# A fused attention and two-layer expert kernel on one core: the order of its instructions taken from a stored table instead of from a scheduler in the kernel

## The chip, the cores and the metric

The kernel runs on one core of a Trainium2 chip. The metric is device time in microseconds (us) from one launch. Several runs of the kernel are timed, and their median is the time; one further execution is recorded by the profiler, and all rows below come from that one.

The engines of the core are named as the profile names them: PE (matrix products), DVE (vector engine), ACT (activations), POOL (GpSimd) and SP, which here only issues DMA transfers. Each engine works through its own list of instructions in a fixed order; between engines they wait for each other by semaphores.

## The reference

Shapes: q, k, v are 4 x 8 x 576 x 64; x is then 2304 tokens x 512; d_ff is 1536.

```
scores = scale * np.matmul(q, k.transpose(0, 1, 3, 2))
mask = (rel >= 0) & (rel < window)                  # window = 64
attn = softmax(np.where(mask, scores, -1e9))
x = (attn @ v), heads joined: 2304 x 512
# layer 1
xn = x / np.sqrt(np.mean(x * x, axis=-1, keepdims=True) + 1e-06) * rms_g
g = xn @ w_gate
x = (g * (1.0 / (1.0 + np.exp(-g))) * (xn @ w_val)) @ w_out
# layer 2
gate = 1.0 / (1.0 + np.exp(-(x @ w_gate2)))
out = (gate * (x @ w_val2)) @ w_out2
```

The weights reach the chip as 64-bit floating point numbers, so the kernel converts them itself.

## The kernel before

**Attention.** There are 36 units of 64 queries for eight heads. A unit is three steps: scores (`st_s`: PE lines 383 to 390, softmax on DVE lines 396 to 400 and 404 to 406, exponentials on ACT line 403), a transposition (`st_tr`, PE line 419 and a copy on ACT line 413) and the product with v (`st_pv`, PE line 455).

**Weights.** A piece of 128 x 1024 weights arrives by one DMA of 1 MB (`w_load`, line 214): 18 pieces for layer 1 and 19 for layer 2. A piece is brought into two fp16 parts, high and low, by `w_max` (the largest magnitude, DVE line 220, and a small all-reduce on POOL line 223), `w_conv` (DVE and ACT, lines 244 to 256) and `w_split` (line 311 or 313 for the high part, line 315 on DVE for the low part). The raw pieces of layer 1 share a few slots: `w_load` of a later piece waits until line 315 has read the earlier piece of its slot.

**Layers.** The tokens go in six blocks of 384, and the 1536 hidden channels in 12 slices of 128. For a layer l, block b and slice f there are:
- `moe_g`, below G(b,f): 12 matmuls of 128 x 384 on line 551, then tanh on ACT (line 563) and in layer 1 a product on DVE (line 565), the last to read the PSUM bank of the matmuls;
- `moe_v`, below V(b,f): 12 matmuls on line 551 into the other of the two banks named `gv`, then a product on DVE (line 576 in layer 1, 578 in layer 2);
- `moe_h`: the hidden values in two fp16 parts (ACT line 592 or 596, DVE line 593 or 597);
- `moe_o`, the output product: for layer 1 twelve matmuls of 128 x 384 on lines 611 to 613, three for each of the four banks named `o`; for layer 2 nine matmuls of 128 x 512 on lines 617 to 619.

Every product needs three matmuls (high by high, high by low, low by high; `mm3`, line 551). A G or V writes into a `gv` bank and so has to wait until the DVE line (565, 576 or 578) that reads the bank's former contents is done. The first two blocks of layer 1 run while its weights are still being converted; their output products come when `w_out` is there. Ahead of each block of layer 1 stands its normalisation (`rms_first` and `split_first` for blocks 0 and 1; for the later ones `rms_sum`, lines 484 to 487 with an all-reduce on POOL, then `rms_scale` lines 521 to 525 and `rms_split` lines 532 and 533). Layer 2 starts a block with `x1_a` and `x1_b` (lines 636 to 655).

**What sets the order.** The program is traced first in the order of the source. Then `arrange` (line 942) puts it in its final order: it groups the matmuls into one tile that follow each other, gives each instruction a price (`price`), lists which instruction must follow which, and lays them down by a list schedule that runs eight times forward and eight times backward. The best of these orders is made firm by a chain of orderings along each engine, DMA issues on SP included. Tiles in pools of more than one buffer are given their buffers beforehand by `plan`; `Pool.tile` (line 54) hands them out.

Of the kernel before, what the change touches and what calls it, by code (L numbers as in the profile page):

```python
# [47 lines left out]
class Pool:  # L48
# [5 lines left out]
    def tile(self, shape, dt, name, tag=None, bufs=1):  # L54
        if bufs == 1:
            return self.pool.tile(shape, dt, tag=tag or name, name=name, bufs=1)
        l = self.asked.setdefault(tag, (bufs, []))[1]
        if self.plan is None:
            a = self.pool.tile(shape, dt, tag=tag, name=name, bufs=bufs)
        else:  # L60
            k = f"{tag}_{self.plan[tag][len(l)]}"
            if k not in self.made:
                self.made[k] = self.pool.tile(shape, dt, tag=k, name=k, bufs=1)
            a = self.made[k]
        l.append(a.name if self.plan is None else k)
        return a
# [820 lines left out]
BYTES = dict(float32=4, int32=4, uint32=4, float16=2, bfloat16=2, uint16=2)  # L887
ROUNDS = 8


def spans(x):
    b = getattr(x, "bass_ap", None)
    if b is None:
        return None
    t, ap, dt = b.tensor, [tuple(p) for p in b.ap], str(b.dtype).split(".")[-1]
    n = math.prod(c for s, c in ap[1:])
    if type(t).__name__ != "Tile":
        return None, 0, 0, 0, 0, n, dt, math.prod(c for s, c in ap) * BYTES.get(dt, 8)
    p0, f0 = divmod(b.offset, ap[0][0])
    sz = BYTES[dt]  # L900
    return t, p0, p0 + ap[0][1], f0 * sz, (f0 + 1 + sum(s * (c - 1) for s, c in ap[1:])) * sz, n, dt, 0


def price(e, i, o, n):

    op = str(i.opcode)
    big = max([x[5] for x in o + n])
    if e == "PE":
        if n[0][6] == "float32":
            t = 218.0 if o[0][5] > 64 else 112.0 if o[0][5] > 1 else 218.0  # L910
        else:
            t = 0.4225 * max(o[0][5], 128)
        return t, t + 160
    if e == "DVE":
        wide = [x for x in n if x[5] == big]
        if big <= 16:
            return 80.0, 165.0
        if op in ("Memset",):
            t = 60 + 0.84 * big
        elif op == "ISA":  # L920
            t = 150 + 0.53 * big
        elif op == "TensorReduce" or len(wide) > 1 or o[0][6] == "uint16" or str(wide[0][0].space).endswith("PSUM"):
            t = 150 + 1.07 * big
        else:
            t = 150 + 0.53 * big
        return t - 80, t
    if e == "Activation":
        t = 210 + 0.95 * big
        if o[0][6] == "uint16":
            t = 200 + 2.24 * big  # L930
        if len(o) > 1:
            t += 190
        return t - 95, t
    if e == "Pool":
        t = 1200.0 if big <= 16 else 2800.0
        return t, t
    by = max(x[7] for x in o + n)
    t = max(by / 300.0, 640.0 if by <= 131072 else 350.0)
    return t, t + 2200.0


def arrange(nc, tc):
    ops, tiles = [], {}
    last = None
    for i in nc.cur_bb.bb.instructions:
# [3 lines left out]
        o = [s for s in map(spans, i.outs) if s]  # L949
        n = [s for s in map(spans, i.ins) if s]  # L950
        occ, lat = price(e, i, o, n)
        key = o[0][0].name if e == "PE" else None
        if e == "PE" and last is not None and last[0] == (key, i.bass_priority - len(ops[last[1]]["ins"])):
            k = last[1]
        else:
            k = len(ops)
            ops.append(dict(e=ENGINES.index(e), ins=[], occ=0.0, lat=0.0, acc=[]))
        g = ops[k]
        g["ins"].append(i)
        g["lat"] = g["occ"] + lat  # L960
        g["occ"] += occ
        g["acc"] += [(True, s) for s in o if s[0] is not None] + [(False, s) for s in n if s[0] is not None]
        last = ((key, ops[k]["ins"][0].bass_priority), k) if e == "PE" else None
    N = len(ops)
    pred = [dict() for _ in ops]
    for k, g in enumerate(ops):
        for w, (t, p0, p1, f0, f1, n, dt, _) in g["acc"]:
            if t.name not in tiles:
                tiles[t.name] = {}
            blocks = tiles[t.name]  # L970
            whole = w and n * BYTES[dt] == f1 - f0
            for b in range(f0 // 1024, (f1 - 1) // 1024 + 1):
                l = blocks.setdefault(b, [])
                keep = []
                for x in l:
                    j, w2, q0, q1, g0, g1 = x
                    hit = j != k and (w or w2) and q0 < p1 and p0 < q1 and g0 < f1 and f0 < g1
                    if hit:
                        pred[k][j] = True
                    a, z = max(g0, b * 1024), min(g1, b * 1024 + 1024)  # L980
                    if not (whole and hit and p0 <= q0 and q1 <= p1 and f0 <= a and z <= f1):
                        keep.append(x)
                keep.append((k, w, p0, p1, f0, f1))
                blocks[b] = keep
    E = [g["e"] for g in ops]
    occ = [g["occ"] for g in ops]
    P = [[(j, ops[j]["lat"] + (0 if E[j] == E[k] == 0 else 35 if E[j] == E[k] else 80 if E[k] == 3 else 45)) if not (E[j] == E[k] == 0) else (j, occ[j]) for j in pred[k]] for k in range(N)]
    S = [[] for _ in ops]
    for k in range(N):
        for j, d in P[k]:  # L990
            S[j].append((k, d))

    def place(P, S, urgency, back):

        todo = [len(p) for p in P]
        heap = [(urgency[k], k) for k in range(N) if not todo[k]]
        heapq.heapify(heap)
        busy = [([], []) for _ in ENGINES]
        at, ready = [0.0] * N, [0.0] * N
        while heap:  # L1000
            _, k = heapq.heappop(heap)
            s0, e0 = busy[E[k]]
            t, d = ready[k], occ[k]
            x = bisect.bisect_right(e0, t)
            while x < len(s0) and t + d > s0[x] + 1e-6:
                t = max(t, e0[x])
                x += 1
            s0.insert(x, t)
            e0.insert(x, t + d)
            at[k] = t  # L1010
            for m, lag in S[k]:


                r = t + lag if not back else t + d + lag - occ[m]
                if r > ready[m]:
                    ready[m] = r
                todo[m] -= 1
                if not todo[m]:
                    heapq.heappush(heap, (urgency[m], m))
        return at, max(at[k] + occ[k] for k in range(N))  # L1020

    topo, todo = [k for k in range(N) if not P[k]], [len(p) for p in P]
    for k in topo:
        for m, _ in S[k]:
            todo[m] -= 1
            if not todo[m]:
                topo.append(m)
# [99 lines left out]
```

## Time and profile before

| | us |
|---|---|
| median of 3 runs | 1020.16 (1020.14 to 1020.78) |
| the profiled execution, its own time | 1016.32 |
| its span, first to last instruction | 1014.5 |
| PE busy | 959.0 (95%) |
| DVE busy | 584.4 (58%) |
| ACT busy | 409.7 (40%) |
| POOL busy | 34.9 (3%) |
| mean granted clock of PE | 0.987 of full speed |

The table is read from the top: the profiled execution took 3.84 us less than the median of the timed ones, and its span lacks 1.8 us of its own time. Busy time is time in which an engine executes; the granted clock is that of PE alone, 1.00 being the full 2.4 GHz. A stretch of the span is described by a row with the busy time of each engine in it, with the number of instructions behind an x.

### The profile page before, as it was taken

Reading aid. Unit: us, or ns where it says so; the run is one execution under the profiler, and the core shown is the slowest. Engines: PE = TensorE matmul, PEld = TensorE weight load, DVE = VectorE, ACT = ScalarE, POOL = GpSimd, SP = SyncE. Lnnn points to the kernel's source line nnn. Section 1 sums busy time; section 2 is a strip of 40 time slices with the busy share of each in tenths; the row PEclk is TensorE's granted clock in tenths of the full one; section 3 lists DMA queues with packets and bytes.
Section 4 is the critical chain, followed back from the end, with each engine's and each line's share of the span. In section 5 each row is a group of like instructions: output and inputs, shape, how many; then the busy total and the mean of one; then the engine's idle time right before and its main releaser. Section 6 shows DMA issues by size and latency. Waiting matters only on the chain.

```text
span 1014.5 us, 14919 instructions
## 1 busy us (share of the span) xinstructions
PE 959.0 (95%) x6176; PEld 583.0 (57%) x6176; DVE 584.4 (58%) x1124; ACT 409.7 (40%) x787; POOL 34.9 (3%) x40
## 2 busy tenths in 40 slices
PE   6667899789999999999999999999999999999998
PEld 6535666456655675675555555555555555555554
DVE  6989998998778888978838813212222222222221
ACT  5478867567342446344414312222222222122122
POOL 0110000100010001001001000000000000000000
PEclk9789999999999999999999999999999999999999
DMA  8455345041530220220013000000000000000000
GB/s 294 122 178 166 116 126 177 11 162 31 197 120 1 52 85 21 95 94 12 1 42 115 12 1 1 1 1 32 1 32 1 1 32 1 1 32 1 1 32 31
DMA packets 43187, 61.54 MB, mean 61 GB/s; under 512 B 23408, under 2 KB 31984, under 8 KB 38640
## 3 DMA queue, kind: packets, MB, share of 16 engines
q1 hardware_dynamic: 43120, 60.60, 18.4%
q8 instruction: 48, 0.79, 0.3%
q14 instruction: 19, 0.16, 0.1%
HBM read 55.87 MB, written 4.72 MB: 60 GB/s over the span
## 4 chain that ended last, share of the span: by engine, by line
PE 80%; DVE 14%; ACT 4%; issue 1%; POOL 0%; DMA 0%; SPq 0%; ACTq 0%; POOLq 0%
PE gv L551 47%; PE o L619 5%; PE o L618 5%; PE o L617 5%; PE o L611 4%; PE o L612 4%; PE o L613 4%; PE at L455 1%; DVE wmax L220 1%; DVE wl L256 1%; DVE th L565 1%; DVE wl L315 1%; PE at L390 1%; PE at L419 1%; PE at L387 1%
## 5 line engine op out<-in xcount | busy, mean ns | idle before, releaser
L551 PE MATMUL gv<-xhl,wl 128*128 128x384 f16 x3456 | 600.8, 329 | 31.4 <-DVE th L565 27.7
L551 PEld LDWEIGHTS <-wl 128*128 128x128 f16 x3456 | 338.6, 98 | 268.3 <-issue 45.5
L597 DVE SCALAR_TENSOR_TENSOR hh<-th,hs,hh 128x384 f16<-128x384 f32 x72 | 44.5, 618 | 238.4 <-ACT hh L596 238.4
L596 ACT ACTIVATE hh<-th,hs 128x384 f16<-128x384 f32 x72 | 44.4, 616 | 256.0 <-PE o L618 243.5
L619 PE MATMUL o<-wl,hh 128*128 128x512 f16 x216 | 81.9, 379 | 0.0
L617 PE MATMUL o<-wl,hh 128*128 128x512 f16 x216 | 81.9, 379 | 0.0
L618 PE MATMUL o<-wl,hh 128*128 128x512 f16 x216 | 81.9, 379 | 0.0
L254 ACT ACTIVATE wl<-wl 128x1024 uint16<-128x1024 uint32 (+1 forms) x32 | 78.8, 2470 | 5.4 <-DVE wl L249 5.3
L578 DVE SCALAR_TENSOR_TENSOR th<-th,gv 128x384 f32<-128x384 f32 x72 | 39.9, 554 | 68.0 <-PE gv L551 68.0
L592 ACT ACTIVATE hh<-th 128x384 f16<-128x384 f32 x48 | 25.1, 523 | 122.8 <-PE o L613 101.4
L563 ACT ACTIVATE th<-gv,tg 128x384 f32<-128x384 f32 x72 | 41.8, 581 | 57.0 <-DVE hh L593 26.3
L611 PE MATMUL o<-hh,wl 128*128 128x384 f16 x192 | 62.8, 327 | 0.0
L612 PE MATMUL o<-hh,wl 128*128 128x384 f16 x192 | 62.7, 327 | 0.0
L613 PE MATMUL o<-hh,wl 128*128 128x384 f16 x192 | 62.6, 326 | 0.0
L563 ACT ACTIVATE th<-gv,be 128x384 f32<-128x384 f32 x72 | 41.8, 580 | 48.9 <-DVE hh L597 43.2
L565 DVE SCALAR_TENSOR_TENSOR th<-th,gv 128x384 f32<-128x384 f32 x72 | 39.7, 551 | 16.9 <-ACT th L563 15.9
L593 DVE TENSOR_TENSOR hh<-th,hh 128x384 f16<-128x384 f32 x48 | 29.6, 617 | 33.0 <-ACT hh L592 32.4
L403 ACT ACTIVATE sm<-sm,nm 128x128 f32<-128x128 f32 x96 | 37.4, 391 | 17.6 <-DVE nm L400 17.5
L220 DVE TENSOR_REDUCE wmax<-wl 128x1 f32<-128x1024 f32 (+1 forms) x37 | 43.5, 1182 | 1.7 <-DMA wl<-in_moe_w_val_dram 1.7
L576 DVE SCALAR_TENSOR_TENSOR th<-th,gv 128x384 f32<-128x384 f32 x72 | 39.4, 547 | 8.2 <-PE gv L551 7.9
L613 PEld LDWEIGHTS <-wl 128*128 128x128 f16 x288 | 28.2, 98 | 18.8 <-issue 0.2
L611 PEld LDWEIGHTS <-wl 128*128 128x128 f16 x288 | 28.3, 98 | 18.3 <-issue 0.2
(168 smaller groups left out, 1040.5 us busy)
## 6 DMA issues: line engine op xcount, KB each, us to landing
wl<-in_moe_w_gate_dram SPq DMA_DIRECT2D x12, 1024.0 KB, 4.8
wl<-in_moe_w_val_dram SPq DMA_DIRECT2D x12, 1024.0 KB, 5.4
wl<-in_moe_w_out_dram SPq DMA_DIRECT2D x11, 1024.0 KB, 4.9
vn<-in_v_dram SPq DMA_DIRECT2D x28, 256.0 KB, 2.8
kt<-in_k_dram SPq DMA_DIRECT2D x15, 256.0 KB, 3.7
qbd<-in_q_dram SPq DMA_DIRECT2D x30, 128.0 KB, 3.7
out_dram<-vn SPq DMA_DIRECT2D x12, 256.0 KB, 2.0
out_dram<-sm SPq DMA_DIRECT2D x6, 256.0 KB, 2.0
```

The lines of the kernel that those rows point to most:

```text
L220: V.tensor_reduce(out=r1[:, i:i + 1], in_=wraw(layer, j + i)[:, :, 1].bitcast(F32), axis=AX.X, op=ALU.max, apply_absolute_value=True)
L254: A.activation(out=r, in_=lo, func=AF.Copy, scale=2.0 ** -29)
L551: T.matmul(pb[:, 0:n], lhsT=w_, rhs=x_, start=(c == 0), stop=(c == m - 1))
L563: A.activation(out=th[:, 0:n], in_=pg[:, 0:n], func=AF.Tanh, scale=sc)
L565: V.scalar_tensor_tensor(out=th[:, 0:n], in0=th[:, 0:n], scalar=1.0, in1=pg[:, 0:n], op0=ALU.add, op1=ALU.mult)
L597: V.scalar_tensor_tensor(out=h[:, 1, 0:n], in0=th[:, 0:n], scalar=sc, in1=h[:, 0, 0:n], op0=ALU.mult, op1=ALU.subtract)
L611: T.matmul(o[c][:, 0:n], lhsT=wh[:, cs], rhs=hi, start=st, stop=False)
L612: T.matmul(o[c][:, 0:n], lhsT=wh[:, cs], rhs=lo, start=False, stop=False)
L613: T.matmul(o[c][:, 0:n], lhsT=wl[:, cs], rhs=hi, start=False, stop=en)
L617: T.matmul(o[t], lhsT=h[:, 0, ts_], rhs=wh, start=st, stop=False)
L618: T.matmul(o[t], lhsT=h[:, 0, ts_], rhs=wl, start=False, stop=False)
L619: T.matmul(o[t], lhsT=h[:, 1, ts_], rhs=wh, start=False, stop=en)
```

## The change

The scheduler inside the kernel (`spans`, `price`, `place` and the rounds of `arrange`) is gone. A table `ORDER`, found beforehand and stored as text, now holds for each engine the order of the groups of instructions, and `arrange` only unpacks it and chains the instructions in that order. The instructions are the same, with the same tiles and addresses. In `Pool.tile`, tiles that have a tag but one buffer (`pT` and `xf`) now also go through the plan. The new file is shorter, but its kernel body stands two lines lower: line 551 before is line 553 now.

```
@@ Pool.tile
-        if bufs == 1:
-            return self.pool.tile(shape, dt, tag=tag or name, name=name, bufs=1)
+        if tag is None:
+            return self.pool.tile(shape, dt, tag=name, name=name, bufs=1)
...
-ROUNDS = 8
...
-def price(e, i, o, n):
...
+ORDER = (
+    'c-n<l349Y}7N7UcB$F?9(kpFg8q(6%UR+vH5JV`TESCs~2rh!+>f%uq4`ex1Ks-2fm$M!Va)}2Zh#ZR?MOKtU%27*8Q+m+!O4^)FGT%-bn#_dy'
...
+)
...
 def arrange(nc, tc):
...
-    for r in range(ROUNDS):
-        at, end = place(P, S, urgency, False)
...
+        key = i.outs[0].bass_ap.tensor.name if e == "PE" else None
+        if e != "PE" or last != (key, i.bass_priority - len(ops[-1][1])):
+            ops.append((e, []))
+            last = (key, i.bass_priority)
+        ops[-1][1].append(i)
...
+    d = zlib.decompress(base64.b85decode(ORDER))
+    n = len(d) // 2
+    assert n == len(ops)
+    seq = list(itertools.accumulate(struct.unpack(f"{n}h", bytes(x for y in zip(d[:n], d[n:]) for x in y))))
...
+    before = None
+    for k in seq:
+        for i in ops[k][1]:
+            if before is not None and before.engine == i.engine:
+                tc.add_manual_dep(i, before.name, mybir.DependencyInfo(mybir.DependencyClass.NoSync, mybir.DependencyReason.DATA), reason="order")
+            before = i
```

Three places show what the table does. In the rows, a name is a tile: `o_...`, `at_...` and `gv_...` are PSUM banks, `xhl_...` the split tokens of a block, `th_...` and `hh_...` hidden values, and `wl_73` and `wl_74` the two large areas that hold weights, raw or converted.

**The start of DVE.** Behind the clearing of buffers, DVE had the softmax of the first units, before:

```order
L396 TENSOR_REDUCE nm_140<-o_134 128x4
L397 TENSOR_SCALAR nm_140<-nm_140 128x4
L396 TENSOR_REDUCE nm_157<-o_151 128x4
L397 TENSOR_SCALAR nm_157<-nm_157 128x4
L404 TENSOR_SCALAR su_143<-su_143 128x4
L405 RECIPROCAL su_143<-su_143 128x4
L396 TENSOR_REDUCE nm_184<-o_174 128x4
L406 TENSOR_TENSOR wl_74<-wl_74,su_143 128x512
```

and now:

```order
L745 MEMSET warm_92 128x1
L764 MEMSET mhalf 128x1
L246 TENSOR_SCALAR wl_73<-wl_74 128x1024
L222 TENSOR_REDUCE wmax_401<-wl_74 128x1
L249 TENSOR_SCALAR wl_73<-wl_73 128x1024
L251 TENSOR_SCALAR wl_74<-wl_74 128x1024
L254 TENSOR_SCALAR wl_74<-wl_74 128x1024
...
L226 TENSOR_SCALAR amax<-amax 128x2
L227 TENSOR_SCALAR pw<-amax 128x2
L230 TENSOR_SCALAR isc<-pw 128x2
L398 TENSOR_REDUCE nm_157<-o_151 128x4
```

The first two weight pieces of layer 1 are converted ahead of the first row of a softmax (line 396, now 398), which comes at place 20. SP follows suit: its first transfer was k, and the first weight piece came at place 11 of its list and the second at 13; now weight pieces stand at places 1, 3, 8 and 12, with k, q and the constants between.

**PE around V(1,10) of layer 1.** `xhl_617` (now `xhl_616`) is block 1 and `xhl_2050` is block 2. Before, V(1,10) followed a G of block 2, and the output products of block 0 began behind it:

```order
L551 MATMUL gv_168<-xhl_2050,wl_73 128x384
L551 LDWEIGHTS wl_73
L551 MATMUL gv_205<-xhl_617,wl_73 128x384
...
L611 LDWEIGHTS wl_73
L611 MATMUL o_174<-wl_74,wl_73 128x384
L612 LDWEIGHTS wl_73
L612 MATMUL o_174<-wl_74,wl_73 128x384
L613 LDWEIGHTS wl_73
L613 MATMUL o_174<-wl_74,wl_73 128x384
```

and now, between G(1,11) and V(1,10):

```order
L553 LDWEIGHTS wl_73
L553 MATMUL gv_168<-xhl_616,wl_73 128x384
L613 LDWEIGHTS wl_73
L613 MATMUL o_134<-wl_74,wl_73 128x384
L614 LDWEIGHTS wl_73
L614 MATMUL o_134<-wl_74,wl_73 128x384
L615 LDWEIGHTS wl_73
L615 MATMUL o_134<-wl_74,wl_73 128x384
L553 LDWEIGHTS wl_73
L553 MATMUL gv_205<-xhl_616,wl_73 128x384
```

Three output matmuls of block 0 stand right ahead of V(1,10), and 66 others stand earlier still: of the 12 x 12 = 144 output matmuls of block 0, none was ahead of V(1,10) and now 69 are. The eight score matmuls of attention unit 20 have also come ahead of it, and G(2,0) has gone behind it. On DVE, 400 instructions had to be done before V(1,10) could start, and now 411.

**DVE where the normalisation of block 3 begins.** Lines 484 to 486 (now 486 to 488) make the squares and their sums, and POOL's all-reduce (line 487) starts right behind them. Line 593 (now 595) makes the low part of a hidden slice. Before:

```order
L484 TENSOR_TENSOR xhl_238<-xf 128x1536
L485 TENSOR_TENSOR xhl_238<-xhl_238 128x768
L486 TENSOR_TENSOR xhl_238<-xhl_238 128x384
L247 TENSOR_SCALAR wl_74<-wl_74 128x1024
L593 TENSOR_TENSOR hh_2269<-th_567,hh_2269 128x384
L565 SCALAR_TENSOR_TENSOR th_567<-th_567,gv_168 128x384
L576 SCALAR_TENSOR_TENSOR th_631<-th_631,gv_205 128x384
```

and now:

```order
L486 TENSOR_TENSOR xhl_238<-xf_538 128x1536
L487 TENSOR_TENSOR xhl_238<-xhl_238 128x768
L567 SCALAR_TENSOR_TENSOR th_480<-th_480,gv_168 128x384
L401 SCALAR_TENSOR_TENSOR sm_437<-at_228,masks 128x512
L488 TENSOR_TENSOR xhl_238<-xhl_238 128x384
L402 TENSOR_REDUCE nm_184<-sm_437 128x4
L249 TENSOR_SCALAR wl_74<-wl_74 128x1024
L578 SCALAR_TENSOR_TENSOR th_630<-th_630,gv_205 128x384
L249 TENSOR_SCALAR wl_74<-wl_74 128x1024
L595 TENSOR_TENSOR hh_2326<-th_630,hh_2326 128x384
```

Between the last sum and the next hidden slice there stood one instruction (line 247), and now there are four.

## Rows read from the trace of the kernel before

A G or a V is a row with line 551 and 12 matmuls, or the first of them where the row holds more or fewer; blocks and slices don't stand in the rows, but follow from the order of the program.

**Rows 1.** The page: busy time of each engine, then the chain that ended last.
```profile
PE 959.0 (95%) x6176; PEld 583.0 (57%) x6176; DVE 584.4 (58%) x1124; ACT 409.7 (40%) x787; POOL 34.9 (3%) x40
...
PE 80%; DVE 14%; ACT 4%; issue 1%; POOL 0%; DMA 0%; SPq 0%; ACTq 0%; POOLq 0%
```

**Rows 2.** Windows by stage: length, busy time by engine (instructions), granted clock, DMA share, GB/s.
```profile
0.00:20.00 20.00, 12.59 (x93) 11.40 (x93) 10.83 (x29) 9.45 (x38) 0.19 (x4) 1.00 0.87 263
...
300.00:510.00 210.00, 206.55 (x1449) 132.40 (x1449) 176.41 (x315) 92.39 (x210) 8.68 (x9) 0.99 0.14 44
...
576.00:1001.00 425.00, 424.95 (x2416) 236.10 (x2414) 96.73 (x171) 94.80 (x160) 0.64 (x1) 1.00 0.03 10
...
40.00:60.00 20.00, 12.58 (x55) 8.27 (x56) 17.20 (x28) 10.52 (x9) 3.67 (x1) 0.72 0.56 162
...
0.00:4.42 4.42, 0.00 (x0) 0.00 (x0) 2.95 (x7) 1.28 (x1) 0.19 (x4) 1.00 0.43 104
```

**Rows 3.** Waits of PE, 0 to 230 us: total, times, longest.
```profile
PE gv L551 <- DVE th L565: 22.7, 12, 5.6
...
PE o L383 <- DMA wl<-const: 6.1, 1, 6.1
```

**Rows 4.** Windows: the stretch up to the start of V(1,10).
```profile
0.00:207.83 207.83, 161.07 (x1220) 113.04 (x1221) 185.29 (x401) 140.93 (x283) 15.38 (x18) 0.94 0.46 145
```

**Rows 5.** Timeline of PE around 61 and 208 us: start, length, what, idle before.
```profile
61.39 4.00 PE L551 MATMUL gv<-xhl,wl 128*128 128x384 f16 x12 [5.56 <-DVE th L565]
...
207.83 2.11 PE L551 MATMUL gv<-xhl,wl 128*128 128x384 f16 x12 [1.74 <-DVE th L576]
209.78 0.33 PE L611 MATMUL o<-wl,wl 128*128 128x384 f16 x1
```

**Rows 6.** Timeline of DVE, 8 to 17 us.
```profile
8.48 0.69 DVE L396 TENSOR_REDUCE nm<-o 128x4 f32<-128x512 f32 x1 [4.06 <-PE o L387]
...
14.47 0.66 DVE L396 TENSOR_REDUCE nm<-o 128x4 f32<-128x512 f32 x1
15.05 0.68 DVE L406 TENSOR_TENSOR wl<-wl,su 128x512 f32<-128x512 f32 x1
...
15.90 0.17 DVE L404 TENSOR_SCALAR su<-su 128x4 f32<-128x4 f32 x1
16.11 0.18 DVE L405 RECIPROCAL su<-su 128x4 f32<-128x4 f32 x1
```

**Rows 7.** Timeline of SP: the first transfer issued.
```profile
0.72 0.68 SPq L345 DMA_DIRECT2D kt<-in_k_dram  x1
```

**Rows 8.** DMA issues of the whole span: count, KB each, median us to landing.
```profile
wl<-in_moe_w_gate_dram SPq DMA_DIRECT2D x12, 1024.0 KB, 4.8
wl<-in_moe_w_val_dram SPq DMA_DIRECT2D x12, 1024.0 KB, 5.4
```

**Rows 9.** The same, issues of the first 25 us.
```profile
wl<-in_moe_w_gate_dram SPq DMA_DIRECT2D x2, 1024.0 KB, 8.9
wl<-in_moe_w_val_dram SPq DMA_DIRECT2D x2, 1024.0 KB, 10.9
```

**Rows 10.** Waits of PE, 215 to 640 us.
```profile
PE gv L551 <- DVE th L565: 4.9, 4, 2.1
```

**Rows 11.** Timeline of all engines, 296.5 to 302 us.
```profile
297.19 2.78 POOL L487 PARTITION_ALL_REDUCE xhl<-xhl  x1 [9.78 <-DVE xhl L486]
297.51 2.02 DVE L593 TENSOR_TENSOR hh<-th,hh 128x384 f16<-128x384 f32 x1
```

**Rows 12.** Timeline of PE, around 301 and 308 us.
```profile
300.79 3.56 PE L551 MATMUL gv<-xhl,wl 128*128 128x384 f16 x12 [2.07 <-DVE th L565]
...
308.15 0.33 PE L613 MATMUL o<-hh,wl 128*128 128x384 f16 x1
308.45 1.78 PE L551 MATMUL gv<-xhl,wl 128*128 128x384 f16 x10
```

**Rows 13.** Timeline of DVE, around 270 us.
```profile
270.56 1.22 DVE L220 TENSOR_REDUCE wmax<-wl 128x1 f32<-128x1024 f32 x1 [1.69 <-DMA wl<-in_moe_w_val_dram]
```

More of the change, by code (lines that the diff above doesn't have):

```diff
@@ L1 @@
-import bisect
-import heapq
+import base64
+import itertools
 import math
+import struct
+import zlib
 from contextlib import ExitStack
@@ L886 @@
 ENGINES = ["PE", "DVE", "Activation", "Pool", "SP"]
-BYTES = dict(float32=4, int32=4, uint32=4, float16=2, bfloat16=2, uint16=2)
-ROUNDS = 8
[L891 to L901, printed above, removed]
@@ L942, in arrange @@
 def arrange(nc, tc):
-    ops, tiles = [], {}
-    last = None
+    ops, last = [], None
     for i in nc.cur_bb.bb.instructions:
@@ L948, in arrange @@
             continue
[L949 to L1027, printed above, removed]
-    assert len(topo) == N, "a circle"
-    tail = [0.0] * N
-    for k in reversed(topo):
-        tail[k] = max([tail[m] + d for m, d in S[k]], default=occ[k])
-    best = None
-    urgency = [float(k) for k in range(N)] if START == "trace" else [-x for x in tail]
-    log = []
-    for r in range(ROUNDS):
-        at, end = place(P, S, urgency, False)
-        log.append(round(end))
-        if best is None or end < best[0]:
-            best = (end, at)
-        back, e2 = place(S, P, [-(at[k] + occ[k]) for k in range(N)], True)
-        log.append(round(e2))
-        urgency = [e2 - back[k] - occ[k] for k in range(N)]
@@ L1043, in arrange @@
-    if VERBOSE:
-        print("arranged", N, log)
-    end, at = best
-    for e in range(len(ENGINES)):
-        before = None
-        for k in sorted((k for k in range(N) if E[k] == e), key=lambda k: (at[k], k)):
-            for i in ops[k]["ins"]:
-                if before is not None:
-                    tc.add_manual_dep(i, before.name, mybir.DependencyInfo(mybir.DependencyClass.NoSync, mybir.DependencyReason.DATA), reason="order")
-                before = i
-    return ops, at, P
-VERBOSE = False
@@ L1057 @@
-START = "tail"
+        key = i.outs[0].bass_ap.tensor.name if e == "PE" else None
[3 more added lines that the diff above has]
+        ops[-1][1].append(i)
+        if e != "PE":
+            last = None
+    d = zlib.decompress(base64.b85decode(ORDER))
+    n = len(d) // 2
+    assert n == len(ops)
+    seq = list(itertools.accumulate(struct.unpack(f"{n}h", bytes(x for y in zip(d[:n], d[n:]) for x in y))))
@@ L1060 @@
+    assert sorted(seq) == list(range(n)) and [ops[k][0] for k in seq] == sorted((e for e, _ in ops), key=ENGINES.index)
+    before = None
[4 more added lines that the diff above has]
+            before = i
 _INS = ['q', 'k', 'v', 'moe_w_gate', 'moe_w_val', 'moe_w_out', 'moe_rms_g', 'moe2_w_gate', 'moe2_w_val', 'moe2_w_out']
```

70 lines of the change are left out of this document (36 added, 34 removed).

## The prediction

> **What bounds the kernel now.** The page comes first. PE is busy for 95% of the span and holds 80% of the chain that ended last; DVE holds 14% of it [rows 1]. So PE is the bound on average, and the question is where it is not. The windows by stage answer that: from 576 to 1001 us PE is busy for 424.95 of 425 us, while it has 12.59 of 20 us at the start [rows 2]. What can be won lies ahead of 576 us, and most of it ahead of 218 us.
>
> Up to 230 us PE's waits are nearly all of one kind: a G or V whose `gv` bank line 565 has not yet read, 22.7 us in 12 waits, the longest 5.6 [rows 3]. DVE explains them: in the first 207.83 us it is busy for 185.29 us, PE for 161.07 and ACT for 140.93 [rows 4]. There DVE is the bound: it converts the weights, and PE can go no faster than DVE lets the banks free. V(1,10) starts at 207.83 us after 1.74 us of waiting for DVE [rows 5]; what PE does from then on waits for little. So the end is set by two numbers: **how late DVE is when V(1,10) may start**, and **how much of PE's work is done by then**.
>
> At full rate twelve matmuls of 128 x 384 start to start take 209.78 - 207.83 = 1.95 us, 162.5 ns each [rows 5]. DVE's price depends on the order too. An instruction that needs nothing of the one before it starts before that one ends (14.47 + 0.66 = 15.13, the next at 15.05: 0.08 us gained); one that needs its direct predecessor starts after it (15.90 + 0.17 = 16.07, the next at 16.11: 0.04 us lost) [rows 6]. Over the whole trace the medians of such pairs are -0.081 us (915 pairs) and +0.035 us (208 pairs). A direct dependence so costs 0.116 us.
>
> **The change part by part.** No instruction is added or taken away, so every term is a shift.
>
> *1. Work moved ahead of V(1,10).* On PE 69 output matmuls of block 0 come ahead of it (69 x 0.1625 = 11.2 us) and 8 score matmuls of unit 20 (0.22 us each in the trace, 1.8), and the 12 of G(2,0) go behind it (1.95): 11.0 us more of PE's work is done by then. On DVE 16 instructions come ahead (two weight pieces' conversion and the softmax of units 18 and 19; 11.25 us by their durations in the trace) and 5 go behind (3.0): 8.2 us more. But of the 400 DVE instructions there 74 waited on their direct predecessor, and of the 411 now 37 do. By start to start that is 8.2 - 11 x 0.081 - 37 x 0.116 = 3.0 us. So PE has 11.0 us less to do behind a gate that opens 3.0 us later: **8.0 us gained**. The bounds are 2.8, if DVE pays full durations, and 11.0. I take 8.0, since the overlap is in the rows.
>
> Here the Trainium skill speaks against the change: "VectorE: DVE Perf Modes", section "The DRAIN you can't avoid", says that the next operation does not start until the pipe is empty and that leaving semaphores out gains nothing. By that this term would be 2.8 us. The trace disagrees with it by the 0.116 us above; the same section also says that an operation which nothing holds starts earlier, and the trace agrees with that.
>
> *2. DVE's start.* In the first 20 us DVE is busy for 10.83, so idle for 9.17 [rows 2]: it waits 4.06 us for the first scores [rows 6], which wait for the constants till 6.1 us [rows 3]. Now it converts weights meanwhile. Its buffers are cleared at 8.48 - 4.06 = 4.42 us [rows 6]. SP's first issue stands at 0.72 [rows 7] and is now a weight piece; over the span such a piece lands 4.8 to 5.4 us after its issue [rows 8], so at 5.5 to 6.1. DVE waits 1.1 to 1.7 us for it, the idle time ahead of 4.42 (4.42 - 2.95 = 1.47 us [rows 2]) stays, and 1.3 us I leave for short waits behind the first piece: 4.2 instead of 9.2 us idle, **5 us gained**. The other bound: in the first 25 us the pieces take 8.9 and 10.9 us [rows 9], which would leave about 1 us. Those stood behind ten other transfers, so I go by the row of the span. PE's own start is later, since k and the constants stand behind the weights; it has 30.2 us of work ahead of G(0,0) where DVE now has 60, so that is covered.
>
> *3. Idle time within DVE's stretch.* From 20 to 207.83 us DVE is idle for 207.83 - 185.29 - 9.17 = 13.4 us [rows 2, 4], in short waits for ACT, PE and POOL. The new order puts other work between most dependent pairs, but five refills of raw weight slots are now used after only 5.8, 7.8, 6.5, 6.5 and 5.9 us of DVE work from the instruction that frees the slot, where before no refill had under 9.7. With landings of 4.8 to 5.4 us they just hold. I take **2 us gained**, of bounds 6 and -3.
>
> *4. Late stops of PE.* From 215 to 640 us PE waits 4.9 us for DVE, 2.07 and 2.08 of it at G(2,8) and G(4,8) [rows 10, 12]. The chain behind: line 593 took 2.02 us instead of 0.56 while POOL's all-reduce ran from 297.19 for 2.78 us [rows 11]; tanh and line 565 came late, and then PE's clock fell, so that the twelve matmuls took 3.56 instead of 2.11 us [rows 5, 12]. Besides, 22 G's between 308 and 576 us started late by the step from 308.15 to 308.45 less 0.1625, 0.14 us [rows 12]: 3.1 us. Together 4.9 + 1.45 + 3.1 = 9.4 us. Now other work stands between the last sum and line 595 in block 3, and there is more PE work between a bank's fill and its next use. What the new order leaves thin are some 20 places in layer 2 with only three matmuls as cover; at 0.14 us each and one half stop they cost 2.8 us at most. I take 2.4: **7 us gained**. Bounds 0 (other DVE instructions now run under the all-reduce; in block 5 a line 595 still directly follows the sums) and 9.4.
>
> **Sum.** 8 + 5 + 2 + 7 = 22 us. Against the profiled execution, 1016.3 - 22 = 994.3 us. The median of the runs lies 3.84 us above that execution; on its basis 1020.2 - 22 = **998 us**.
>
> **The rivals.**
>
> *A. Only the moved work counts.* The first weights land as slowly as in [rows 9], the refills eat the inner gains, and the late stops come back under other instructions, as half of them may. Then 8 + 1 + 0 + 0 = 9 us: 1011. For it: PE's waits go back to DVE again and again, so whatever frees one exposes the next. Against it: DVE's work ahead of any PE place is at most 30 us more than PE's own now, where it was 36 at V(1,10).
>
> *B. DVE pays full durations.* Then term 1 is 2.8 instead of 8: 1003 us. For it: 0.04 us are lost, not gained, at each direct dependence [rows 6], and 37 of them are left; against it: the 915 pairs that overlap. The section of the Trainium skill that is named under term 1 would bring it about.
>
> *C. Slower: weights come too late.* The five short refills stand between 25 and 210 us, where DVE is the bound, so each us of a late piece is a us of the end. In the trace of before DVE once waited 1.69 us for a piece that stood behind other transfers [rows 13], and in the crowded start a piece took 10.9 us [rows 9]. A refill that takes both, 12.6 us, against a mean cover of 6.5, costs 6.1 us; five of them 30 us: 998 + 30 = 1028 us. It decides once the five together lose over 22 us, which is at landings of 10.9. Against it: the landings of the span [rows 8].
>
> *D. The change does nothing much.* The order of the table may be one that hardly differs where it counts, or the renamed tiles and 81 more waiting instructions on ACT take it back (at the 0.04 us of a dependent step [rows 6], 3.2 us, on an engine that is idle for 67 of 207.83 us [rows 4]). Then 1017 to 1021.
>
> PE's clock is a risk on both sides: it is granted 0.72 between 40 and 60 us [rows 2], where twelve matmuls take 4.00 us [rows 5]; as long as DVE is the bound there, this costs nothing.
>
> **How the numbers follow.** About 2 us, 0.2%, is what a measurement of this kernel can tell from no change. My forecast, with its own range of 985 to 1004, has a chance of 0.56; A 0.20; B 0.10; C 0.09; D 0.05. Faster is the forecast with A and B, 0.86; the same is D, 0.05; slower is C, 0.09. The low end, 985, takes terms 2 to 4 at their good bounds (6 + 6 + 9, with term 1 at 8, is 29: 991) and term 1 at 11 with some 3 us more for waits that vanish altogether. The high end, 1012, takes in A. Left out are C and D and a little at the low end.
>
> **What would show it right or wrong.** In the new profile the first G starts near 64 us instead of 47.6, yet V(1,10) starts near 204 us with 11 us more of PE's work done; DVE is idle for about 4 of the first 20 us and for some 15 us up to V(1,10), not 22.5; a G with 2 us of waiting right behind POOL's long all-reduce is rare; and from 576 us on PE has no gap. Term 1 is wrong if DVE's steps don't get shorter start to start. Rival C shows as DVE waiting for DMA by line 222 in the waits, and A as PE waits of over 5 us behind 215 us.

## The result and the profile after

| | before | changed |
|---|---|---|
| median of four runs each | 1020.25 us (1020.14 to 1020.78) | 996.5 us (995.46 to 997.68) |
| ratio, 95% interval | | 0.9767 (0.9750 to 0.9783) |
| the profiled execution, its own time | 1016.32 | 997.35 |
| its span | 1014.5 | 995.6 |

The change makes the kernel 23.75 us faster by the medians and 19.0 us by the profiled executions. Executions of one kernel scatter by some us here (the kernel before took 1015.97 to 1020.78 us over the whole study, and its profiled execution is among the fastest), so totals are compared by medians and ratios below, and stretches within one profile.

The page of the changed kernel, first the busy times, then the chain that ended last:

```profile
PE 958.7 (96%) x6176; PEld 587.7 (59%) x6176; DVE 579.0 (58%) x1124; ACT 404.9 (41%) x787; POOL 31.7 (3%) x40
...
PE 89%; DVE 5%; DMA 3%; ACT 2%; issue 1%; SPq 1%; DVEq 0%; ACTq 0%
```
PE is as busy as before, in 19 us less; of the chain, DVE's share fell from 14% to 5% [rows 1].

The windows by stage, with the columns of [rows 2], then the stretches up to the first G and up to V(1,10):

```profile
0.00:20.00 20.00, 8.52 (x51) 7.75 (x52) 16.80 (x30) 7.05 (x15) 0.92 (x5) 1.00 0.99 301
...
300.00:510.00 210.00, 209.65 (x1474) 133.19 (x1473) 174.98 (x313) 92.99 (x194) 11.96 (x10) 1.00 0.14 43
...
576.00:990.00 414.00, 413.38 (x2322) 226.93 (x2320) 90.68 (x160) 91.76 (x155) 0.35 (x1) 1.00 0.03 10
...
0.00:204.78 204.78, 174.18 (x1293) 125.74 (x1294) 188.63 (x414) 146.97 (x302) 11.08 (x18) 0.91 0.52 164
0.00:68.85 68.85, 40.11 (x304) 35.21 (x305) 60.50 (x143) 45.84 (x102) 4.39 (x9) 0.75 0.69 214
```
In the first 20 us DVE is idle for 3.20 us, not 9.17, and PE does less (8.52 us, not 12.59). From 300 to 510 us PE lacks 0.35 us of being always busy, not 3.45 [rows 2]. In layer 2 it lacks 0.62 us, where before it lacked 0.05 (the ends of matmuls are modelled, so short delays show only in part). Up to V(1,10), DVE is busy for 188.63 of 204.78 us; before it was 185.29 of 207.83 [rows 4].

The timeline of PE at the first G (36 matmuls without a gap), at V(1,10) and at V(1,11):

```profile
68.85 6.01 PE L553 MATMUL gv<-xhl,wl 128*128 128x384 f16 x36
...
204.78 2.11 PE L553 MATMUL gv<-xhl,wl 128*128 128x384 f16 x12
...
207.66 0.65 PE L553 MATMUL gv<-xhl,wl 128*128 128x384 f16 x3
```
V(1,10) starts 3.05 us earlier than before [rows 5], with 11.05 us more of PE's work done: 14.1 us are won by then. The first G, at 68.85 us, is 21 us later than in the kernel before.

Waits of PE, from 68 to 230 us and then from 215 us to the end:

```profile
PE gv L553 <- DVE th L567: 1.8, 2, 1.5
...
PE gv L553 <- DVE th L578: 1.5, 1, 1.5
PE gv L553 <- DVE th L567: 0.3, 1, 0.3
```
Before, the first kind took 22.7 us up to 230 us and 4.9 us behind it [rows 3, 10].

The windows from 40 us to V(1,10) show when PE became the bound:

```profile
40.00:60.00 20.00, 12.01 (x75) 10.65 (x75) 17.35 (x45) 15.92 (x33) 0.00 (x0) 0.50 0.45 144
60.00:68.85 8.85, 7.59 (x62) 6.21 (x62) 7.54 (x26) 4.84 (x7) 1.09 (x1) 0.59 0.41 151
68.85:100.00 31.15, 29.65 (x220) 19.92 (x220) 28.75 (x63) 27.25 (x60) 0.77 (x3) 1.00 0.48 153
100.00:140.00 40.00, 39.91 (x308) 28.07 (x306) 38.25 (x92) 32.71 (x57) 1.45 (x3) 0.96 0.48 152
140.00:204.78 64.78, 64.51 (x468) 42.53 (x467) 61.14 (x121) 41.16 (x85) 4.47 (x4) 1.00 0.39 123
```
From 68.85 us on PE is busy for 134.07 of 135.93 us, and DVE for 128.14. Both engines are nearly full there. Most of what PE lost by V(1,10), it lost ahead of 68.85 us, where DVE was busy for 60.50 us and PE's clock fell to half.

**The account of lost time.** The table takes the start of a PE instruction less the full-rate time of all PE work ahead of it (162.5 ns for a 128 x 384 matmul, 216 ns for 128 x 512, and so on): the time that PE had lost when so much of its work was done. It is worked out from the trace and the order of each kernel; the other columns belong to runs below.

| PE work done, us | before | changed | new to 112, then old | new to 272, then old | old to 286, then new | old layer 2 and one swap |
|---|---|---|---|---|---|---|
| 60 | 48.1 | 47.5 | 48.1 | 48.2 | 50.8 | 45.5 |
| 160 | 65.7 | 51.9 | 65.3 | 52.6 | 68.4 | 48.6 |
| 220 | 66.7 | 53.2 | 66.3 | 53.9 | 70.3 | 49.9 |
| 540 | 80.6 | 58.9 | 80.5 | 69.0 | 76.4 | 54.8 |
| 900 | 80.5 | 61.7 | 80.4 | 68.9 | 79.2 | 54.7 |

Three parts can be read from the first two columns: 13.5 us are won by 220, another 8.2 us between 220 and 540 (the rest of layer 1), and 2.9 us are lost again in layer 2. Against this execution of the kernel before, nothing is won by 60: the gain is made between 60 and 160 us of work.

The first row depends on the execution, though: the old order had lost 50.8 us by 60 in another one (old to 286), and the changed kernel, run again, had lost 45.4. From 60 to 900 its two executions lost 14.2 and 14.6 us, the kernel before 32.4. So gains of an order are best read from 60 on.

### The profile page after: what moved, and what is told of

It is laid out like the page before. It is cut to its first block, busy times and chain, and to the rows that moved or that the text cites. A ratio compares the mean times of both kernels' runs of the same rounds, so it can differ in the third digit from the quotient of the medians.

```text
span 995.6 us, 14971 instructions
## 1 busy us (share of the span) xinstructions
PE 958.7 (96%) x6176; PEld 587.7 (59%) x6176; DVE 579.0 (58%) x1124; ACT 404.9 (41%) x787; POOL 31.7 (3%) x40
## 4 chain that ended last, share of the span: by engine, by line
PE 89%; DVE 5%; DMA 3%; ACT 2%; issue 1%; SPq 1%; DVEq 0%; ACTq 0%
PE gv L553 55%; PE o L619 5%; PE o L621 5%; PE o L613 5%; PE o L620 5%; PE o L615 4%; PE o L614 4%; PE at L457 2%; PE at L389 1%; DMA wl<-in_moe_w_val_dram 1%; PE at L391 1%; PE at L392 1%; DMA wl<-in_moe_w_gate_dram 1%; PE at L421 1%; DMA qbd<-in_q_dram 1%
## 5 line engine op out<-in xcount | busy, mean ns | idle before, releaser
L553 PE MATMUL gv<-xhl,wl 128*128 128x384 f16 x3456 | 590.4, 326 | 4.4 <-DVE th L567 2.1
L553 PEld LDWEIGHTS <-wl 128*128 128x128 f16 x3456 | 337.5, 98 | 236.0 <-issue 10.3
L256 ACT ACTIVATE wl<-wl 128x1024 uint16<-128x1024 uint32 (+1 forms) x32 | 78.6, 2474 | 14.6 <-DVE wl L251 14.5
L615 PEld LDWEIGHTS <-wl 128*128 128x128 f16 x288 | 28.2, 98 | 18.6
L613 PEld LDWEIGHTS <-wl 128*128 128x128 f16 x288 | 28.3, 98 | 17.4
L614 PEld LDWEIGHTS <-wl 128*128 128x128 f16 x288 | 28.2, 98 | 17.1
```

The lines of the kernel that those rows point to most:

```text
L256: A.activation(out=r, in_=lo, func=AF.Copy, scale=2.0 ** -29)
L553: T.matmul(pb[:, 0:n], lhsT=w_, rhs=x_, start=(c == 0), stop=(c == m - 1))
L613: T.matmul(o[c][:, 0:n], lhsT=wh[:, cs], rhs=hi, start=st, stop=False)
L614: T.matmul(o[c][:, 0:n], lhsT=wh[:, cs], rhs=lo, start=False, stop=False)
L615: T.matmul(o[c][:, 0:n], lhsT=wl[:, cs], rhs=hi, start=False, stop=en)
```

## The experiments

All are the changed file with another table; the instructions are the same in every one, and none leaves out work. My theory was that of the prediction: an early part (DVE's start and work moved ahead of V(1,10)) and a late part, which add up.

**Is it the order alone?**

```
 ORDER = (
-    the table of the change
+    the order of the kernel before, written as a table
 )
```

> The order of the kernel before, written as a table into the changed kernel; everything else of the change stays (the unpacking, the renamed one-buffer tiles). My theory, that only the order of the instructions counts: 1020.2 us, within 1.5. Rival, that the renamed tiles and the waits that come with them take part in the gain or cost something: off from 1020.2 by 3 us or more, either way.

Measured: 1017.51 us beside 1018.51 for the kernel before, ratio 0.9995 (0.9980 to 1.0011). (The expected 1020.2 was the median of another series.) The renamed tiles cost and gain nothing that can be measured. That rules out my rival D's second half, and lets the old order stand for the kernel before in what follows.

**The two halves, first attempt.** The table takes one order up to a time, with all that this needs, and the rest in the other.

```
+    new order for what it starts before 232 us; then the old order        (first part)
+    old order for what it starts before 235 us; then the new order        (last part)
```

> The new order for all that the changed kernel starts in its first 232 us (with all that this needs), then the rest in the order of before. My theory, two separate gains: what PE has won by 232 us (13.7 us) stays, the late part (8.0 us won in layer 1, 2.9 lost in layer 2) goes: 1020.2 - 13.7 = 1006.5 us, 1004 to 1009. Rival 1, all of the gain is made ahead of 232 us: 997. Rival 2, the early gain is taken back because the late order of before makes PE wait for the same DVE work a little later: over 1012.

> The reverse: the order of before for its first 235 us, then the rest in the new order. My theory: the late part alone, 8.0 won and 2.9 lost, 1020.2 - 5 = 1015 us, 1012 to 1017. Rival 1, the late order only works when DVE is ahead early: 1019 or slower. Rival 2, most of the gain is late: under 1008.

Measured: first part 1010.5 us, ratio 0.9917 (0.9889 to 0.9946); last part 1018.55 us, ratio 0.9999 (0.9987 to 1.0011). Both missed. PE's waits behind the seam show why. In the first part, on the timeline:

```profile
244.99 3.46 PE L553 MATMUL gv<-xhl,wl 128*128 128x384 f16 x12 [6.00 <-DVE th L567]
```
and in the last part, in the list of waits behind 215 us:

```profile
PE at L457 <- ACT pT L415: 3.6, 3, 2.0
```
Each kernel waits right at its seam, since one order there expects work that the other had not done yet. So the totals measured the seam as well, and told nothing on the question.

**The two halves, at a better seam.** The seam now lies where both orders have done nearly the same work.

```
+    new order for what it starts before 272 us; then the old order
+    old order for what it starts before 286 us; then the new order
```

> The new order for all that the changed kernel starts in its first 272 us, then the order of before. At 232 us the two orders had done different things (24 us of PE and DVE work that only one of them had behind it), and the first attempt lost 9.3 us of PE's time right at that seam; at 272 us (286 us in the kernel before) they differ by 6 us. My theory, separate gains: 13.5 us are won by then and stay, the late part is lost as before: 23.7 - 8.0 + 2.9 = 18.6, or by stretches 13.5 to 18 us under the kernel before, ratio 0.982 to 0.987. Rival, that the early gain is taken back by the late order wherever the seam lies: ratio 0.99 or more, as in the first attempt.

> The order of before for its first 286 us, where the two orders differ by 6 us of work, then the new order. My theory: the late part alone, 14.2 us of PE's late time become 5.1 in layer 1, and 2.8 are lost in layer 2: 5 to 6.3 us under the kernel before, ratio 0.9938 to 0.995. Rival, that the late order needs DVE ahead: ratio 0.999 or more, as in the first attempt with the seam at 235 us.

Measured: new to 272, 1004.05 us beside 1018.58, ratio 0.9855 (0.9834 to 0.9876); old to 286, 1012.24 us beside 1018.81, ratio 0.9941 (0.9921 to 0.9962). Both are as expected: 14.5 and 6.6 us, in sum 21.1, where the whole change gave 22.4 us beside the second of them. The late part's 6.6 is an upper figure: its executions had a mean granted clock of 0.981 to 0.988, those of the kernel before beside them 0.978 to 0.983. By the account of lost time, from 60 us of work on, the early part gains 11.7 us and the late one 4.0, in sum 15.7 of 18.2. In the main the two are separate gains.

**Within the early part: the output products.**

```
 PE, around V(1,10) of layer 1
-    69 output matmuls of block 0 ahead of V(1,10)
     V(1,10)
+    the 69 output matmuls
```

> The new order, but on PE the 69 output matmuls of block 0 that it had moved ahead of V(1,10) stand right behind V(1,10) again; DVE, ACT, POOL and SP are as in the changed kernel. In its trace DVE lets V(1,10) go at 203.1 us and V(1,11) at 207.5, and PE reaches them at 204.8 and 207.7. My theory, that these matmuls fill PE while DVE is behind: PE waits at V(1,10) until about 203.1, then has 11.2 us of outputs ahead of V(1,11): about 9.5 us lost, 996.5 + 9.5 = 1006 us, 1003 to 1008. Rival, that the gain comes from DVE's early start and PE would have had the matmuls' time anyway: 996 to 998.

Measured: 1008.05 us (1005.02 to 1010.26), 11.6 us over the changed kernel, ratio to the kernel before 0.9889 (0.9868 to 0.9909). On PE's timeline the waits for DVE are back:

```profile
187.31 2.11 PE L553 MATMUL gv<-xhl,wl 128*128 128x384 f16 x12 [1.68 <-DVE th L567]
194.62 3.89 PE L553 MATMUL gv<-xhl,wl 128*128 128x384 f16 x12 [5.19 <-DVE th L567]
...
205.13 2.11 PE L553 MATMUL gv<-xhl,wl 128*128 128x384 f16 x12 [0.99 <-DVE th L578]
```
By the account of lost time, from 60 to 900 us of work, this kernel lost 23.7 us and the changed one 14.2, which is 9.5 more. So whether all of the matmuls' 11.2 us were lost, or the 9.5 that I expected, is not settled. The rows do settle the place: not V(1,10) alone waits, but already two G's ahead of it, and at the second the twelve matmuls took 3.89 us instead of 2.11. My expectation named the wrong place, and the mechanism stands: these matmuls fill PE while DVE is behind.

**Within the early part: DVE's start.**

```
+    new order for what it starts before 112 us; then the old order
```

> The new order for all that the changed kernel starts in its first 112 us, a place where the two orders have done nearly the same work (the new one 6.8 us of DVE and 2.8 us of PE more), then the order of before. My theory: this is the start's gain alone, 6 to 7 us under the kernel before, ratio 0.993 to 0.994. Rival 1, an earlier DVE start is lost again at the next wait: ratio 0.998 or more. Rival 2, the start is what the whole early gain comes from: 13 us, ratio 0.987.

Measured: 1015.87 us (1012.78 to 1018.9), ratio 0.9970 (0.9956 to 0.9985), beside 1018.81: 3 us, half of what I expected. (The account of lost time compares single executions and shows no gain by 900, 80.4 against 80.5.) Windows of this kernel:

```profile
0.00:20.00 20.00, 8.57 (x46) 7.70 (x47) 16.84 (x30) 7.09 (x15) 0.92 (x5) 1.00 0.99 303
...
112.00:150.00 38.00, 33.79 (x236) 22.66 (x233) 30.56 (x79) 22.24 (x43) 0.37 (x1) 1.00 0.34 110
```
the same stretch of the changed kernel:

```profile
112.00:150.00 38.00, 37.91 (x286) 27.07 (x284) 36.41 (x91) 28.54 (x54) 1.80 (x4) 0.96 0.48 154
```
and in the list of DVE's waits up to 208 us:

```profile
DVE th L567 <- ACT th L565: 7.7, 8, 2.6
```
DVE does start early (16.84 us busy of 20) and has then 7.4 us without work between 112 and 150 us. In the old order it meets the products of G's that PE has not come to; 7.7 us go in such waits, where the kernel before has some 2. So an early start of DVE does not give its full price without an order behind it that gives both engines work. The reverse, the moved output products without the early start, was not run.

**The late stops: POOL's all-reduce.** On DVE, blocks 3 and 5, with the lines of the changed file (block 3 shown):

```
 L487 TENSOR_TENSOR xhl_238<-xhl_238 128x768
+L595 TENSOR_TENSOR hh_2256<-th_566,hh_2256 128x384
 L488 TENSOR_TENSOR xhl_238<-xhl_238 128x384
-L249 TENSOR_SCALAR wl_74<-wl_74 128x1024
-L595 TENSOR_TENSOR hh_2256<-th_566,hh_2256 128x384
 L567 SCALAR_TENSOR_TENSOR th_566<-th_566,gv_168 128x384
 L578 SCALAR_TENSOR_TENSOR th_630<-th_630,gv_205 128x384
+L249 TENSOR_SCALAR wl_74<-wl_74 128x1024
```

> The order of before, but on DVE in blocks 3 and 5 of layer 1 the low part of the hidden slice goes ahead of the last sum and the 128 x 1024 weight instruction behind the two products that read PSUM, so that nothing with two SBUF inputs and no large SBUF-only instruction stands between POOL's long all-reduce and the products that PE waits for. My theory, that the all-reduce holds such instructions up: PE waits some 0.5 instead of 2.1 us at G(2,8) and G(4,8), and the slow clock behind the first stop goes: 4 us, 2.5 to 5.6, under the order of before (ratio 0.994 to 0.998). Rival, that PE waits there for another reason: ratio 0.999 to 1.001, the stops stay.

Measured: 1016.0 us beside 1018.58, ratio 0.9978 (0.9964 to 0.9991). The timeline of this kernel:

```profile
296.81 0.56 DVE L595 TENSOR_TENSOR hh<-th,hh 128x384 f16<-128x384 f32 x1 [0.47 <-ACT hh L594]
297.29 0.55 DVE L488 TENSOR_TENSOR xhl<-xhl 128x384 f32<-128x384 f32 x1
...
298.02 0.55 DVE L567 SCALAR_TENSOR_TENSOR th<-th,gv 128x384 f32<-128x384 f32 x1 [0.18 <-ACT th L565]
298.04 2.74 POOL L489 PARTITION_ALL_REDUCE xhl<-xhl  x1 [10.69 <-ACT th L565]
...
298.62 2.11 PE L553 MATMUL gv<-xhl,wl 128*128 128x384 f16 x12
...
298.95 1.30 DVE L249 TENSOR_SCALAR wl<-wl 128x1024 int32<-128x1024 int32 x1
...
480.11 2.11 PE L553 MATMUL gv<-xhl,wl 128*128 128x384 f16 x12 [1.62 <-DVE th L567]
```
Line 595 takes 0.56 us, G(2,8) starts without a wait at 298.62, and what now stands under the all-reduce, line 249, takes 1.30 us instead of the 0.69 that it takes elsewhere. Both stops of [rows 10, 12] are gone. In block 5 another came behind them (1.62 us at 480.11: the normalisation's chain, which now starts earlier, stands ahead of line 595 there), so the gain is 2.6 us, at the lower end.

The changed kernel has the same thing in other clothes. Its timeline:

```profile
291.10 2.74 POOL L489 PARTITION_ALL_REDUCE xhl<-xhl  x1 [15.84 <-DVE xhl L488]
...
291.42 1.90 DVE L249 TENSOR_SCALAR wl<-wl 128x1024 int32<-128x1024 int32 x1
...
293.24 0.54 DVE L578 SCALAR_TENSOR_TENSOR th<-th,gv 128x384 f32<-128x384 f32 x1
...
293.83 1.46 PE L553 MATMUL gv<-xhl,wl 128*128 128x384 f16 x8 [1.54 <-DVE th L578]
```
Line 249 under the all-reduce takes 1.90 us, and the product of V(2,5) stands behind it; PE waits 1.54 us.

**Layer 2, and a faster kernel.**

```
+    new order through layer 1 (its first 563 us); then the old order
```

> The new order through layer 1 (all that the changed kernel starts in its first 563 us), then layer 2 in the order of before. In the changed kernel PE starts 14 times late by 0.13 to 0.25 us in layer 2, where three output matmuls cover the release of a bank; the order of before has nine there. My theory: those 2.8 us come back, 996.5 - 2.8 = 993.7 us. Rival, that the old layer 2 does not fit behind the new layer 1 and waits at the seam: 996 or slower.

and then, besides, on DVE in block 3:

```
 L402 TENSOR_REDUCE nm_184<-sm_437 128x4
-L249 TENSOR_SCALAR wl_74<-wl_74 128x1024
 L578 SCALAR_TENSOR_TENSOR th_630<-th_630,gv_205 128x384
+L249 TENSOR_SCALAR wl_74<-wl_74 128x1024
 L249 TENSOR_SCALAR wl_74<-wl_74 128x1024
```

> As the kernel with the old layer 2, and on DVE in block 3 the product of V(2,5) goes ahead of a 128 x 1024 weight instruction that took 1.90 instead of 0.69 us under the all-reduce in the changed kernel (PE waited 1.54 us for it). My theory: 1.5 us less than the kernel with the old layer 2, some 992.2 us, the fastest of all. Rival, that the wait moves to the next instruction: as that kernel.

Measured: 994.05 us (992.56 to 995.28), ratio 0.9759 (0.9739 to 0.9778), with the old layer 2; 991.43 us (990.52 to 994.98), ratio 0.9740 (0.9719 to 0.9761), with the swap too. The first came as expected. The second is by its median the fastest kernel of the study, some 5 us under the changed one, but the two intervals overlap, and the swap explains little of the step between them: the spans of the two profiled executions differ by 4.8 us, and 4.4 of these were lost ahead of 60 us of PE's work (49.9 and 45.5), where both have the same order. From 60 to 900 the two lost 9.6 and 9.2 us. The layer 2 of the second kernel, and its all-reduce of block 3:

```profile
560.00:985.00 425.00, 424.95 (x2402) 234.74 (x2400) 93.95 (x166) 95.31 (x160) 0.64 (x1) 1.00 0.03 10
```
```profile
287.20 2.74 POOL L489 PARTITION_ALL_REDUCE xhl<-xhl  x1 [15.22 <-DVE xhl L488]
...
288.07 0.56 DVE L578 SCALAR_TENSOR_TENSOR th<-th,gv 128x384 f32<-128x384 f32 x1 [0.47 <-PE gv L553]
...
288.55 1.95 DVE L249 TENSOR_SCALAR wl<-wl 128x1024 int32<-128x1024 int32 x2
...
292.52 2.11 PE L553 MATMUL gv<-xhl,wl 128*128 128x384 f16 x12 [0.59 <-DVE th L578]
```
PE lacks 0.05 us in layer 2, and the product of V(2,5) (288.07) no longer waits behind line 249. PE's wait there, 0.9 us with the old layer 2 alone, is gone, and one of 0.59 us came a little later: the rival, that the wait moves on, holds in the main.

**What a direct dependence costs.** The changed kernel was run once more beside it.

> The changed kernel once more, as the measure for the run with direct dependences on the same chip: 995 to 998 us.

At 23 places on DVE, of this kind:

```
 L398 TENSOR_REDUCE nm_140<-o_151 128x4
-L251 TENSOR_SCALAR wl_74<-wl_74 128x1024
 L399 TENSOR_SCALAR nm_140<-nm_140 128x4
+L251 TENSOR_SCALAR wl_74<-wl_74 128x1024
```

> The new order, but on DVE at 23 places ahead of V(1,10) two neighbours are exchanged so that an instruction again stands right behind the one it needs: 69 of the 411 instructions then wait on their direct predecessor instead of 37, and no instruction comes more than one place later. My theory, that each such dependence costs DVE 0.116 us: 3.7 us more DVE time, and with PE's slack of 0.1 to 0.2 us at G(1,10) and V(1,11) 2.5 to 3.7 us more for the kernel than the changed one. Rival, that DVE drains behind every instruction anyway (the rule of the Trainium skill's page VectorE: DVE Perf Modes, section The DRAIN you can't avoid): no difference, within 1 us.

Measured: 996.43 us for the changed kernel, 997.32 (996.8 to 999.95) with the dependences back; ratios 0.9779 (0.9760 to 0.9799) and 0.9794 (0.9774 to 0.9815). The time settles nothing: 0.9 us lies inside the intervals, under the 2.5 that I expected, and within what the rival allows. The traces do settle the price of one place. Up to 204 us, 69 instructions that needed their direct predecessor started 0.035 us behind its end, by the median, and 318 others 0.082 us ahead of it; in the changed kernel 37 and 342 did, at the same two values. They do not bear out the sum, 32 x 0.116 = 3.7 us: DVE's instructions 141 to 411, from about the first G to V(1,10), took 130.9 us without their waits of over 0.07 us, and 129.1 in both executions of the changed kernel. That is 1.8 us more; why not 3.7 stays open. The waits of PE from 68 to 230 us, with the dependences back and then without:

```profile
PE o L508 <- DVE xhl L507: 2.0, 1, 2.0
PE gv L553 <- DVE th L567: 0.3, 1, 0.3
```
```profile
PE gv L553 <- DVE th L567: 0.7, 2, 0.4
```
PE waits 2.3 us instead of 0.7, and by the account it lost 16.4 us from 60 to 900 us of work, where the changed kernel lost 14.2 and 14.6.

## Why the prediction was right, and where it was not

Predicted were 998 us, 985 to 1012, with faster at 0.86; measured are 996.5. The sum of the terms was made against the profiled execution: 22 us predicted, 19.0 measured.

One reading behind it was too wide. Up to 230 us PE's waits in the kernel before sum to 46.7 us, and the 22.7 that the prediction calls nearly all are half of them; 17.6 lie ahead of the first G. No term rests on it.

**Term 1 (8.0 us).** PE had 11.05 us more behind it at V(1,10), as counted, and DVE was busy for 188.63 - 185.29 = 3.3 us longer, predicted 3.0. It is right in size, and putting the matmuls back cost 11.6 us, or 9.5 by the account. Rival B falls: DVE was busy 3.3 us longer, not 8.2, and the prices of 0.035 and -0.082 us hold in three traces. The rule of the Trainium skill behind it ("VectorE: DVE Perf Modes", "The DRAIN you can't avoid": the next operation waits until the pipe is empty, semaphores or not) does not agree with these traces, where 342 instructions started 0.082 us ahead of the end before them, by the median; what the section adds, that an operation which nothing holds starts earlier, does agree.

**Term 2 (5 us).** The first weight was there at 5.83 us, 1.39 us after DVE was ready for it, and DVE had its first scores at 14.17 us, having converted weights till then:

```profile
5.83 0.69 DVE L246 TENSOR_SCALAR wl<-wl 128x1024 f32<-128x1024 f32 x1 [1.39 <-DMA wl<-in_moe_w_gate_dram]
...
14.17 0.69 DVE L398 TENSOR_REDUCE nm<-o 128x4 f32<-128x512 f32 x1 [0.17 <-PE o L389]
```
DVE's idle time in 20 us fell by 9.17 - 3.20 = 6.0 us. So the size was right, and the step that failed is that I added it as a term of its own: run alone, the new start was worth 3 us, since the old order behind it made DVE wait for PE. With the new order behind it and only the outputs put back, 14.5 - 11.6 = 2.9 us of the early part were left, near 6.0 + 0.4 (term 3) - 3.3 = 3.1. So term 2 holds only together with the order of term 1; whether term 1 needs the early start, no run shows.

**Term 3 (2 us).** Between 20 us and V(1,10) DVE was idle for 204.78 - 188.63 - 3.20 = 12.95 us; 13.4 before. It gave 0.4. Rival C is what took the rest, in small; among DVE's waits up to 215 us stand

```profile
DVE wmax L222 <- DMA wl<-in_moe_w_gate_dram: 1.9, 1, 1.9
...
DVE wmax L222 <- DMA wl<-in_moe_w_val_dram: 1.2, 1, 1.2
```
which is 3.1 us of waiting for refilled weights. It never came near the 22 us from which C would have decided. The size of this term changes from execution to execution: when the changed kernel ran again, V(1,10) started at 202.77 us,

```profile
0.00:202.77 202.77, 173.63 (x1293) 124.41 (x1294) 188.43 (x414) 146.89 (x302) 11.07 (x18) 0.91 0.52 166
```
DVE was idle for 3.06 us in the first 20, and for 202.77 - 188.43 - 3.06 = 11.28 us from there on, 0.8 of them for a refill. There term 3 gave 2.1 us, as predicted.

In the first execution the three together: 6.0 + 0.4 - 3.3 = 3.1 us earlier at V(1,10), as the row shows (3.05), and 11.05 of work: 14.1, predicted 15.

**Term 4 (7 us).** By the account of lost time 8.2 us were won in layer 1, where I had hoped for nearly all of 9.4, and 2.9 lost in layer 2, where I took 2.4, and 2.8 at most for layer 2 and half a stop together: 5.3 in all. That sum was wrong, since 20 x 0.14 is 2.8 by itself and leaves nothing for the half stop. So what is missing is the stop at 293.83 us: I had named the chance that other DVE instructions would come under the all-reduce, and it is not in the sum. In layer 2 PE starts 14 times late by 0.13 to 0.25 us; one of them:

```profile
755.32 0.38 PE L621 MATMUL o<-wl,hh 128*128 128x512 f16 x1
755.78 1.95 PE L553 MATMUL gv<-xhl,wl 128*128 128x384 f16 x11
```
The last of three matmuls starts at 755.32, the next V at 755.78 instead of 755.54. I gave 0.14 us each for 20 places; it is nearly the same sum. My list of signs contradicted that term, though: it said that PE would have no gap from 576 us on.

**What bounds the kernel.** I had V(1,10) as the gate that counts. It is so in the kernel before. In the changed one PE runs without notable waits from its first G on, so most of what is lost is lost ahead of 68.85 us. I had put that G near 64 us. In the last 8.85 us ahead of it PE was busy for 7.59 at a granted clock of 0.59, so a slow clock may cost time there. My sentence that it costs nothing while DVE is the bound overlooks that a low clock can make DVE wait for PE. (Its row, the 4.00 us at 61.39, also lies behind the window that it names.) The old order shows it, in the kernel before and then in the last-part run, which has the same order up to 235 us:

```profile
28.00:47.60 19.60, 12.63 (x98) 11.49 (x99) 18.56 (x45) 9.35 (x10) 1.78 (x1) 0.77 0.36 107
```
```profile
28.00:47.60 19.60, 14.80 (x86) 13.33 (x87) 15.63 (x40) 7.33 (x9) 1.77 (x1) 0.50 0.28 75
...
49.98 4.37 PE L553 MATMUL gv<-xhl,wl 128*128 128x384 f16 x13
```
With the clock granted at 0.50 instead of 0.77, DVE is busy for 15.63 of these 19.60 us, not 18.56, and the first G starts at 49.98 us, not 47.59, though DVE had the same 37.1 us of work ahead of it. The old-to-286 run agrees (0.50, 50.22), and its delay stays: 68.4 us lost by 160 us of work, where the kernel before has 65.7. What the clock costs in the changed kernel, no run isolates.

Rival A (only the moved work counts, 1011 us) falls with the 996.5 us, and with the run that is old to 286 us, where the late part gave 6.6 us by itself (4.0 by the account).

**The medians.** The median came out 1.5 us under the prediction, though the profiled execution lay 3 us over its own forecast of 994.3. The prediction carried the 3.84 us between execution and median over to the changed kernel, as if they belonged to it. They did not: the profiled execution of before lay 3.9 us under its median, that of the changed kernel 0.9 over. To that extent it is luck that 998 fits so well.

## What to carry to other kernels

When two engines feed each other in order, count for each gate how much work each has ahead of it: the gain comes from work that one engine can do while the other is behind, and an early start of the slower one only pays if the order behind it keeps it from waiting. Look also at what stands under a POOL operation on the vector engine, and put there what reads PSUM. To test parts of an order, splice two orders at a place where both have done the same work; elsewhere the seam is what is measured.

## What was not expected of the hardware

- While POOL's all-reduce of 128 x 384 runs (2.74 us), some DVE instructions are held and some not. Line 593 with two SBUF inputs took 2.02 instead of 0.56 us [rows 11], line 249 with one large SBUF input 1.90 or 1.30 instead of 0.69; the products that read PSUM took their usual 0.54 to 0.55. What an instruction reads does not decide alone: in the changed kernel line 595, the former 593, took its usual time late in an all-reduce:

```profile
374.53 2.74 POOL L489 PARTITION_ALL_REDUCE xhl<-xhl  x1 [15.15 <-PE gv L553]
...
376.67 0.55 DVE L595 TENSOR_TENSOR hh<-th,hh 128x384 f16<-128x384 f32 x1
```
The Trainium skill's page "SBUF — State Buffer", section "SBUF: two separate sides", says that a GpSimd operation and a DVE operation with two SBUF inputs, or in a mode with two ports, lock one pair of ports against each other for the whole instruction. As far as the profile's rough spans on POOL go, the rows agree in that line 593 is held; they do not agree in how long, since it ended at 299.53 us and the all-reduce at 299.97 [rows 11], nor does line 595 at 376.67.
- PE's clock was granted at 0.50, all of it at the lower level of 1.2 GHz, between 40 and 60 us, where PE was busy for 12.01 of 20 us; before, it was 0.72 with 12.58 us [rows 2].
